# Attention in blocks of 32 queries by 64 keys ahead of an MLP: both heads of a pair in one pass, weights converted two blocks at a time, first stage in a written order

## The chip, the core and the metric

The kernel runs on one core of a Trainium2 chip. Times are device microseconds of that core, from launch to end, as the median of several executions. The core has a matrix engine (TensorE, PE in the profile, with its weight loads counted apart as PEld), three engines for everything else (VectorE or DVE, ScalarE or ACT, GpSimd or POOL), and an engine that issues the transfers (SyncE or SP). Each works through its own list of instructions in order; they wait for each other by semaphores.

## The reference: what is computed

Eight batches of eight heads, 576 tokens, 64 channels a head. Heads 0 to 3 see the last 32 tokens, heads 4 to 7 every fourth of the last 128. The heads' outputs side by side are a matrix of 4608 tokens by 512, and go through an MLP of 512 to 2048 to 512.

```python
rel = pos[:, None] - pos[None, :]
mask_plain = (rel >= 0) & (rel < window)                                    # window 32
mask_dil = (rel >= 0) & (rel < window * dilation) & (rel % dilation == 0)   # dilation 4
scores = scores - np.max(scores, axis=-1, keepdims=True)
attn = np.exp(scores)
attn = attn / (np.sum(attn, axis=-1, keepdims=True) + 1e-09)
...
h = x @ w_in
g = np.where(pos, h, np.where(neg, 0.0, (h + beta) ** 2 / (4.0 * beta)))   # pos: h >= 1, neg: h <= -1
return (g @ w_out).astype(np.float32)
```

The MLP's weights come as 64-bit floats.

## The kernel before

**MLP.** The 4608 tokens are nine tiles of 512, the 2048 hidden channels 16 blocks of 128. Activations and weights are held as two fp32r parts (high and rest), and each product of 128x128 by 512 columns is three matmuls: high by high, rest by high, high by rest. Layer 1 (line 396) takes 12 matmuls for a tile and a block, layer 2 (line 433) 12 as well: 3456 in all. A step s is one tile and one block: `layer1(s)`, then `layer2(s - 2)`. Between the two and behind the second, `run(2s)` and `run(2s + 1)` put in the pieces of attention that `place` has assigned to these slots. Between the layers the activation of a block is three passes on DVE (lines 410, 415, 419) and two on ACT (413, 416).

**Attention.** Heads 4 to 7 are re-arranged on the host so that a window is 32 neighbours there too. Queries go in tiles of 96, and each tile is scored against 128 keys, of which 32 to a query are in its window. The first 16 heads (two batches) are scored as plain fp32 matmuls (line 204), two heads in two row halves of the array. For the 48 later heads `split` cuts q and k into high and rest (lines 138 to 143), and line 227 scores a tile by one fp32r matmul of 96x256. DVE adds the mask (line 246), and a custom instruction for each tile (line 175) scales and takes the extreme at once; ACT makes the exp of each tile, with its sum (line 252); POOL multiplies by the inverse sums (line 285). DVE transposes the result in blocks of 32 (line 300, six for each head); for the first 16 heads PE does it (line 324). Line 358 multiplies by the values, 12 fp32 matmuls for a pair of heads, in two column halves. `store_x` then writes the high part (line 342, ACT) and the rest (line 343, DVE) into the tiles xh and xl, three of each, which layer 1 reads. A tile of 512 tokens is complete when the pair of heads 6 and 7 of its last batch is stored.

**Weights.** `fetch` brings a block (512 KB), and `weights` makes its two parts: ACT (line 115), ACT or DVE (121 or 123), a join of the two on DVE (126), the high part on ACT (131), the rest on POOL (132). 32 blocks are converted, in the steps of the first tile for the most part.

**What sets the order.** PE and SP run in program order all through. DVE, ACT and POOL are ordered by a scheduler, by priorities. `issue_after` holds the conversion of a block behind marks in ACT's and DVE's work. Eight heads are scored and transposed, and most of their values made, before layer 1 begins.

Of the kernel before, what the change touches and what calls it, by code (L numbers as in the profile page):

```python
# [6 lines left out]
F32 = mybir.dt.float32  # L23
# [4 lines left out]
ALU = mybir.AluOpType  # L28

# [3 lines left out]
QT, NQ = 96, 6  # L33
# [4 lines left out]
NF = DF // 128  # L38
NC = DM // 128
EPS = 1e-09  # L40
# [4 lines left out]
def body(ctx, tc, q, k, q2, k2, v, mask, eye, w_in, w_out, out):  # L45
# [7 lines left out]
    msk = const.tile([QT, 3, 128], F32, name="msk")  # L53
    ident = const.tile([QT, QT], F32, name="ident")
    consts = const.tile([128, 16], F32, name="consts")
    half_t = consts[:, 0:1]
    pts = [const.tile([128, NQ, QT], F32, name=f"pt{i}") for i in range(2)]
# [3 lines left out]
    nhead = B * H  # L61
    native = 2 * H

    spare = [f"{w}{f}" for f in range(NF // 2, NF) for w in ("wi", "wo")]

    def borrow(name):
        return pool.tile([128, 2 * DM], F32, tag=spare.pop(0), name=name)

    def load_pair(n):

        if 0 < n < H:
            qr, kr = borrow(f"qr{n}")[:, :S], borrow(f"kr{n}")[:, :KPAD]
        else:
            tags = ("qs", "kk") if n % 4 else ("qr", "kr")
            qr = pool.tile([128, S], F32, tag=tags[0], name=f"qr{n}")
            kr = pool.tile([128, KPAD], F32, tag=tags[1], name=f"kr{n}")
        nc.sync.dma_start(out=qr, in_=q[n // 2])
        nc.sync.dma_start(out=kr, in_=k[n // 2])
        for j in range(2):
            r = slice(64 * j, 64 * j + 64)  # L80
            heads[n + j] = dict(qs=qr[r], ks=kr[r])

    def load(n):
        qr = pool.tile([128, S], F32, tag="qr", name=f"qr{n}")
        kr = pool.tile([128, KPAD], F32, tag="kr", name=f"kr{n}")
        nc.sync.dma_start(out=qr, in_=q2[n - native])
        nc.sync.dma_start(out=kr, in_=k2[n - native])
        heads[n] = dict(qr=qr, kr=kr)

    def load_values(n):  # L90
        if 0 < n < H:
            vt = borrow(f"vt{n}")[:, : 2 * NQ * D]
        else:
            vt = pool.tile([128, 2 * NQ * D], F32, tag="vt", name=f"vt{n}", bufs=2)
        nc.sync.dma_start(out=vt, in_=v[n // 2])
        vt = vt.rearrange("p (j t d) -> p j t d", j=2, t=NQ)
        for j in range(2):
            heads[n + j]["vt"] = vt[:, j]

    wi, wo, raws = {}, {}, {}  # L100

    def fetch(f, src, name):

        raw = pool.tile([128, 2 * DM], U32, tag=f"{name}{f}", name=f"{name}_raw{f}")
        nc.sync.dma_start(out=raw, in_=src[:, f].bitcast(U32))
        raws[name, f] = raw

    def weights(f, w, name):

        raw = raws.pop((name, f))  # L110
        words = raw.rearrange("p (n x) -> p n x", x=2)
        low, high = words[:, :, 0], words[:, :, 1]
        m = pool.tile([128, DM], U32, tag="m", name=f"{name}_m{f}", bufs=3)

        nc.scalar.activation(
            out=m.bitcast(F32), in_=high.bitcast(F32), func=AF.Prelu, scale=2.0**-112, alpha=2.0**32
        )
        if name == "wi":

            top = raw.bitcast(U8).rearrange("p (n x) -> p n x", x=8)[:, :, 3]  # L120
            nc.scalar.activation(out=low, in_=top, func=AF.Copy, scale=1.0 / 32, bias=-31.0 / 64)
        else:
            nc.vector.tensor_scalar(
# [27 lines left out]
    def bank(n):  # L151

        if n > H:
            return "att", 2
# [527 lines left out]
```

## Time and profile before

| | |
|---|---|
| time, median of 3 executions | 948.66 us (948.19 to 948.94) |
| the profiled execution: span from the first to the last instruction | 945.8 us |
| granted TensorE clock over the span | 0.986 |
| layer 2 on PE, high part of the activations (line 433) | 385.8 us in 1152 |
| layer 1 on PE, high part (line 396) | 362.2 us in 1152 |
| exps on ACT (line 252) | 140.6 us in 360 |
| transposes on DVE (line 300) | 106.0 us in 288 |

For the profiled execution the profile has a span and no time of its own; the median of the other executions lies 2.9 us above that span. A row of the groups reads: line, engine, operation, what is written from what, shapes, count | busy us, mean ns of one | idle time before and what ended it. A matmul in fp32 leaves two records, each with a weight load; one in fp32r leaves one. Matmuls overlap in the array, so a record's length is more than the distance to the next start.

### The profile page before, as it was taken

The page shows a single profiled execution, that of the slowest core. Times are in us where ns is not written, and L with a number is a line of the kernel's source. Part 1 is how long each engine was busy: PE and PEld are TensorE (multiplying, and loading weights), DVE is VectorE, ACT ScalarE, POOL GpSimd, SP SyncE. Part 2 cuts the span into 40 slices and gives each one's busy share as a digit, 9 for nine tenths or more (in the row PEclk, how much of TensorE's full clock was granted, in tenths as well). Part 3 has the DMA queues.
Part 4 walks back from the last instruction along what each step waited for, and adds up shares of the span by engine and source line. Part 5 has one row for each costly group of instructions (what it writes and reads, how often), then busy time and mean ns, then how long its engine had stood idle before and what let it go on. Part 6 is the DMA issues. An engine that isn't in the chain of part 4 may idle for free.

```text
span 945.8 us, 14337 instructions
## 1 busy us (share of the span) xinstructions
PE 920.9 (97%) x4822; PEld 748.4 (79%) x4822; DVE 681.1 (72%) x1979; ACT 493.8 (52%) x1392; POOL 230.9 (24%) x148
## 2 busy tenths in 40 slices
PE   6679999999999999999999999999999999999998
PEld 5557788888888888888888888888888888888886
DVE  6788887888887788788887888888877643334333
ACT  6777876555565555555555555555655332222222
POOL 3454552222222222222222222222222000000000
PEclk8879999999999999999999999999999999999999
DMA  9961101322232113222322123222321010001001
GB/s 347 407 239 51 44 27 43 113 69 69 69 113 62 49 57 110 69 69 69 97 86 58 57 66 113 69 69 69 113 62 50 1 45 1 0 1 45 1 1 44
DMA packets 31017, 73.85 MB, mean 78 GB/s; under 512 B 3520, under 2 KB 3808, under 8 KB 30944
## 3 DMA queue, kind: packets, MB, share of 16 engines
q1 hardware_dynamic: 30944, 72.94, 23.7%
q8 instruction: 38, 0.62, 0.3%
q14 instruction: 35, 0.29, 0.1%
HBM read 63.49 MB, written 9.44 MB: 77 GB/s over the span
## 4 chain that ended last, share of the span: by engine, by line
PE 91%; ACT 4%; DVE 4%; DMA 1%; issue 1%; DVEq 0%; ACTq 0%
PE acc L433 41%; PE h L396 40%; PE o L358 4%; PE s L227 4%; ACT c L252 2%; DVE wi_m L126 1%; DMA wi_raw<-w_in 1%; DVE wo_m L126 1%; PE s L201 1%; DVE c L175 0%; ACT wi L131 0%; PE s L204 0%; PE t L324 0%; ACT xh L342 0%; DVE h L415 0%
## 5 line engine op out<-in xcount | busy, mean ns | idle before, releaser
L433 PE MATMUL acc<-wo,gh 128*128 128x512 f32 x1152 | 385.8, 396 | 4.1 <-ACT pt L326 4.1
L396 PE MATMUL h<-xh,wi 128*128 128x512 f32 x1152 | 362.2, 395 | 5.0 <-ACT xh L342 4.9
L433 PEld LDWEIGHTS acc<-wo,gh 128*128 128x128 f32 x1152 | 217.3, 189 | 52.8 <-ACT pt L326 4.3
L396 PEld LDWEIGHTS h<-xh,wi 128*128 128x128 f32 x1152 | 210.1, 189 | 47.4 <-ACT xh L342 5.3
L396 PE MATMUL h<-xl,wi 128*128 128x512 f32 x576 | 227.6, 395 | 0.0
L433 PE MATMUL acc<-wo,gl 128*128 128x512 f32 x576 | 226.0, 392 | 0.0
L252 ACT ACTIVATE c<-c 96x128 f32<-96x128 f32 x360 | 140.6, 393 | 117.9 <-DVE c L175 117.9
L143 POOL TENSOR_TENSOR kk<-kr,kk 128x608 fp32r<-128x608 f32 x48 | 95.3, 1985 | 422.8 <-ACT kk L139 422.8
L413 ACT ACTIVATE y<-y,consts 128x512 f32<-128x512 f32 x144 | 104.2, 724 | 123.6 <-DVE y L410 123.6
L416 ACT CAST gh<-h 128x512 fp32r<-128x512 f32 x144 | 84.6, 587 | 126.8 <-PE acc L433 122.1
L410 DVE TENSOR_SCALAR y<-h 128x512 f32<-128x512 f32 x144 | 99.3, 690 | 61.1 <-PE h L396 59.9
L415 DVE TENSOR_TENSOR h<-h,y 128x512 f32<-128x512 f32 x144 | 100.6, 699 | 52.8 <-ACT y L413 51.5
L396 PEld LDWEIGHTS h<-xl,wi 128*128 128x128 f32 x576 | 108.5, 188 | 25.5 <-DVE xl L343 0.2
L419 DVE TENSOR_TENSOR gl<-h,gh 128x512 fp32r<-128x512 f32 x144 | 98.8, 686 | 39.7 <-ACT gh L416 39.4
L433 PEld LDWEIGHTS acc<-wo,gl 128*128 128x128 f32 x576 | 108.8, 189 | 21.3
L300 DVE STREAM_TRANSPOSE pt<-c 32x192 f32<-32x192 f32 x288 | 106.0, 368 | 5.8
L246 DVE TENSOR_TENSOR c<-s,msk 96x256 f32<-96x256 f32 (+1 forms) x168 | 61.5, 377 | 39.6 <-PE s L227 38.6
L285 POOL TENSOR_TENSOR c<-c 96x768 f32<-96x768 f32 x56 | 82.6, 1477 | 21.0 <-DVE c L284 20.7
L175 DVE CUSTOM_DVE_ANT_0 c<-s,c 96x128 f32<-96x128 f32 x288 | 70.6, 281 | 1.0
L252 ACT ACTIVATION_READ_ACCUMULATOR c<-c 96x1 f32 x360 | 68.0, 189 | 0.0
L342 ACT CAST xh<-o 128x288 fp32r<-128x288 f32 (+8 forms) x112 | 38.4, 380 | 47.2 <-PE o L358 28.7
L227 PEld LDWEIGHTS s<-kk,qs 128*96 128x96 f32 x288 | 46.4, 161 | 15.7
(57 smaller groups left out, 632.8 us busy)
## 6 DMA issues: line engine op xcount, KB each, us to landing
kr<-k_in SPq DMA_DIRECT2D x56, 304.0 KB, 3.3
qr<-q_in SPq DMA_DIRECT2D x56, 288.0 KB, 2.8
vt<-v_in SPq DMA_DIRECT2D x32, 384.0 KB, 4.0
wi_raw<-w_in SPq DMA_DIRECT2D x16, 512.0 KB, 9.4
wo_raw<-w_in SPq DMA_DIRECT2D x16, 512.0 KB, 9.8
out<-out SPq DMA_DIRECT2D x32, 256.0 KB, 3.7
out<-outs SPq DMA_DIRECT2D x4, 256.0 KB, 2.0
msk<-mask_in SPq DMA_DIRECT2D x1, 144.0 KB, 3.6
```

The source lines that it names most:

```text
L143: nc.gpsimd.tensor_tensor(out=kk[:, 1], in0=hd["kr"], in1=kk[:, 0].bitcast(F32), op=ALU.subtract)
L227: PE.matmul(out=sv[:, t - t0], lhsT=hd["qs"][:, t * QT : (t + 1) * QT], rhs=hd["ks"][:, :, t * QT : t * QT + 128], start=True, stop=True,)
L252: last["act"] = nc.scalar.activation(out=c[:, t], in_=c[:, t], func=AF.Exp, bias=st[:, 0, t : t + 1], scale=-1.0, accum_out=st[:, 1, t : t ...
L285: nc.gpsimd.tensor_tensor(out=c, in0=c, in1=spread(st[:, 2]), op=ALU.mult)
L300: nc.vector.transpose(out=pt[r : r + 32, :, 32 * g : 32 * g + 32], in_=c[32 * g : 32 * g + 32, :, r : r + 32],)
L396: PE.matmul(out=hp, lhsT=wi[f][:, w, 128 * c : 128 * c + 128], rhs=x[:, c], start=c == 0 and i == 0, stop=c == NC - 1 and i == len(terms) - 1,
L410: nc.vector.tensor_scalar(out=y, in0=hp, scalar1=-1.0, scalar2=1.0, op0=ALU.max, op1=ALU.min)
L413: nc.scalar.activation(out=y, in_=y, func=AF.Square, bias=half_t, scale=0.5)
L415: activated = nc.vector.tensor_tensor(out=hp, in0=hp, in1=y, op=ALU.max)
L416: copied = nc.scalar.copy(out=gh, in_=hp)
L419: nc.vector.tensor_tensor(out=gl, in0=hp, in1=gh.bitcast(F32), op=ALU.subtract)
L433: PE.matmul(out=acc[m], lhsT=g[:, r], rhs=wo[f][:, w], start=f == 0 and i == 0, stop=f == NF - 1 and i == len(terms) - 1,)
```

## The change

- Queries go in blocks of 32, and each is scored against its 64 keys. The 18 blocks of a head are 18 fp32 matmuls of 64 rows by 32 columns with 64 moving columns; three blocks lie side by side in three column places, the two heads of a pair in the two row halves (line 126 of the new kernel). No head is split into high and rest any more.
- The softmax runs over both heads at once, 96 x 768: mask added (DVE, line 152 or 159), maximum (DVE, 170), subtraction (POOL, 174), one exp (ACT, 178), sums (DVE, 182), inverse, product (POOL, 188).
- The first eight pairs are transposed on PE as matmuls with an identity and multiplied by their values in 36 matmuls of 64x32; the 24 others are transposed on DVE, six instructions of 32x384 for a pair (line 211), and keep their 12 matmuls, now in turns between the heads.
- q and k of a pair come in one transfer, once, not doubled.
- Weights are fetched and converted two blocks at a time, 1024 columns a pass; all get the second ACT pass.
- Up to the first layer's start the order is written out for PE, SP, DVE, ACT and POOL. From there on, PE and SP are in program order as before, the others scheduled.

```diff
-QT, NQ = 96, 6
+QB, NB = 32, S // 32
+KW = 64
+EARLY = 8
...
+        for b in range(NB):
+            t, g = divmod(b, 3)
+            for j in range(2):
+                r = slice(64 * j, 64 * j + 64)
                 PE.matmul(
-                    out=sv[:, t - t0],
-                    lhsT=heads[m]["qs"][:, t * QT : (t + 1) * QT],
-                    rhs=heads[m]["ks"][:, t * QT : t * QT + 128],
+                    out=sps[j][QB * g : QB * g + QB, KW * t : KW * t + KW],
+                    lhsT=hd["q"][r, QB * b : QB * b + QB],
+                    rhs=hd["k"][r, QB * b : QB * b + KW],
...
+    def largest(n):
+        nc.vector.tensor_reduce(out=heads[n]["st"][:, 0], in_=heads[n]["c"], op=ALU.max, axis=AX.X)
+    def minus_largest(n, engine=nc.gpsimd):
+        c = heads[n]["c"]
+        engine.tensor_tensor(out=c, in0=c, in1=spread(n, 0), op=ALU.subtract)
+    def exp(n):
+        c = heads[n]["c"]
+        last["act"] = nc.scalar.activation(out=c, in_=c, func=AF.Exp, scale=1.0 / 8.0)
+    def sums(n):
+        c, st = heads[n]["c"], heads[n]["st"]
+        nc.vector.tensor_reduce(out=st[:, 1], in_=c, op=ALU.add, axis=AX.X)
+        nc.scalar.activation(out=st[:, 1], in_=st[:, 1], func=AF.Copy, bias=EPS)
+    def inverses(n, engine=nc.gpsimd):
+        c, st = heads[n]["c"], heads[n]["st"]
+        nc.vector.reciprocal(out=st[:, 2], in_=st[:, 1])
+        engine.tensor_tensor(out=c, in0=c, in1=spread(n, 2), op=ALU.mult)
...
+    def transpose(n):
+        c = heads[n]["c"].rearrange("p j t x -> p (j t) x")
+        pt = pts.rearrange("p j t i -> p (j t) i")
+        for g in range(3):
+            for h in range(2):
+                r = 32 * (g + h)
+                nc.vector.transpose(
+                    out=pt[r : r + 32, :, 32 * g : 32 * g + 32],
+                    in_=c[32 * g : 32 * g + 32, :, 32 * h : 32 * h + 32],
+                )
...
+        if n < EARLY:
+            for turn in range(2):
+                for i in range(half):
+                    for j in range(2):
+                        part = turn ^ j
+                        r = slice(64 * j, 64 * j + 64)
+                        at = half * part + i
+                        PE.matmul(
+                            out=ops[part][r, QB * i : QB * i + QB],
+                            lhsT=hd["v"][r, at],
+                            rhs=hd["pt"][r, QB * at : QB * at + QB],
...
+    def scaled(name, u):
+        ms[name, u] = pool.tile([128, 2, DM], F32, tag="m", name=f"m_{name}{u}", bufs=2)
+        nc.scalar.activation(
+            out=flat(ms[name, u]), in_=words_of(name, u)[1].bitcast(F32),
+            func=AF.Prelu, scale=2.0**-112, alpha=2.0**32,
+        )
...
+    for n in range(4, NP):
+        u = 8 * (n - 4) - 4
+        if n > 4:
+            place(u, lambda n=n: scores_step(n))
+            place(u + 1, lambda n=n: masks(n), lambda n=n: largest(n), lambda n=n: minus_largest(n))
+            place(u + 2, lambda n=n: exp(n))
+            place(u + 3, lambda n=n: sums(n))
+            place(u + 4, lambda n=n: inverses(n))
+        if n < EARLY:
+            place(u + 7, lambda n=n: transpose_pe(n))
         else:
+            place(u + 5, lambda n=n: transpose(n))
+        place(u + 10, lambda n=n: values_step(n))
+        place(u + 11, lambda n=n: stores(n))
...
+    with tc.manual_schedule(engines={eng.PE, eng.SP, eng.DVE, eng.Activation, eng.Pool}):
+        scores(0)
+        load_qk(4)
+        largest(0)
+        minus_largest(0, nc.vector)
+        exp(0)
...
+        layer1(0, 0, range(2))
+        layer1(0, 1, range(2))
+        values(2, (0, 1), store=False)
+        parts("wi", 1)
+        exp(4)
+        stores(2)
+        sums(4)
+        values(3, (2, 3), store=False)
+        fetch(("wi", 7), ("wo", 7))
+        scaled("wo", 0)
+        inverses(4)
+        stores(3)
+        top_bytes("wo", 0)
+        joined("wo", 0)
+        parts("wo", 0)
```

Three places of the order that follows. First PE in the long run, where a pair's scores come: before, two score matmuls (s from kk and qs) stand between the layers, here at the end of layer 1's block 4 (h from xh, xl and wi) and ahead of layer 2 (acc from wo, gh and gl).

```order
L396 MATMUL h_4_2959<-xh_853,wi_668 128x512 x2
L396 MATMUL h_4_2959<-xl_854,wi_668 128x512
L227 MATMUL s_2_2980<-kk_2871,qs_2870 96x256 x2
L433 MATMUL acc_0_2848<-wo_721,gh_2_2835 128x512
L433 MATMUL acc_0_2848<-wo_721,gl_2_2836 128x512
```

After, PE at the like place, at the end of layer 1's block 10:

```order
L377 MATMUL h_10_2176<-xh_381,wi_1048 128x512 x2
L377 MATMUL h_10_2176<-xl_382,wi_1048 128x512
L126 MATMUL s_2198<-qk_2027 32x64 x36
L412 MATMUL acc_0_1818<-wo_1131,gh_8_2116 128x512
L412 MATMUL acc_0_1818<-wo_1131,gl_8_2117 128x512
```

All 36 score matmuls of a pair stand in one place; before, they were six twos in six places.

Second, DVE in the first stage. Before, among the tiles' reduces (line 175, two instructions for each of the first heads' tiles, c from s and msk) the first sums and inverses stand where the scheduler put them:

```order
L175 ISA c_174<-s_4_194,msk 96x128
L175 ISA c_174 96x1
L271 TENSOR_SCALAR sums<-c_115 96x6
L175 ISA c_176<-s_4_195,msk 96x128
L175 ISA c_176 96x1
L175 ISA c_176<-s_4_195,msk 96x128
L175 ISA c_176 96x1
L276 RECIPROCAL c_115<-sums 96x6
```

After, DVE's first rows behind the memset are those of the written order (c_100 is pair 0, c_155 pair 1, qkc_74 pair 2):

```order
L152 TENSOR_TENSOR c_100<-s_101,msk 96x768
L170 TENSOR_REDUCE c_100<-c_100 96x12
L174 TENSOR_TENSOR c_100<-c_100 96x768
L150 TENSOR_TENSOR c_155<-s_0_156,msk 96x384
L150 TENSOR_TENSOR c_155<-s_1_157,msk 96x384
L170 TENSOR_REDUCE c_155<-c_155 96x12
L182 TENSOR_REDUCE c_100<-c_100 96x12
L150 TENSOR_TENSOR qkc_74<-s_2_200,msk 96x384
L150 TENSOR_TENSOR qkc_74<-s_3_201,msk 96x384
L187 RECIPROCAL c_100<-c_100 96x12
L170 TENSOR_REDUCE qkc_74<-qkc_74 96x12
L182 TENSOR_REDUCE c_155<-c_155 96x12
```

A pair's mask, maximum and sum are now single passes over both heads, and pair 1's mask and maximum stand between pair 0's subtraction and its sum.

Third, DVE where the last pair of a token tile is stored. Before (y, h and gl are the activation of block 15; xl_1935 is the tile that layer 1 takes up next, xl_2929 the one behind it; pt from c are the next head's transposes):

```order
L284 RECIPROCAL c_3552<-c_3552 96x6
L410 TENSOR_SCALAR y_15_3636<-h_15_3623 128x512
L343 TENSOR_TENSOR xl_1935<-o_0_3644,xh_1934 128x2x80
L415 TENSOR_TENSOR h_15_3623<-h_15_3623,y_15_3636 128x512
L343 TENSOR_TENSOR xl_1935<-o_1_3655,xh_1934 128x2x80
L343 TENSOR_TENSOR xl_2929<-o_0_3644,xh_2928 128x2x64
L300 STREAM_TRANSPOSE pt_67<-c_3552 32x6x32 x6
L343 TENSOR_TENSOR xl_2929<-o_1_3655,xh_2928 128x2x64
```

After, at the same boundary (xl_1889 is the tile that is taken up next, xl_2735 the one behind it; pts from c are the next pair's transposes):

```order
L394 TENSOR_SCALAR y_15_3318<-h_15_3305 128x512
L187 RECIPROCAL c_3250<-c_3250 96x12
L398 TENSOR_TENSOR h_15_3305<-h_15_3305,y_15_3318 128x512
L252 TENSOR_TENSOR xl_1889<-o_3326,xh_1888 128x2x80
L211 STREAM_TRANSPOSE pts<-c_3250 32x12x32 x6
L252 TENSOR_TENSOR xl_2735<-o_3326,xh_2734 128x2x64
L402 TENSOR_TENSOR gl_15_3320<-h_15_3305,gh_15_3319 128x512
L252 TENSOR_TENSOR xl_1889<-o_3326,xh_1888 128x2x80
L252 TENSOR_TENSOR xl_2735<-o_3326,xh_2734 128x2x64
```

The second store into the next tile stands behind the transposes, a store into the tile after it, and gl; before, both stood ahead of the transposes.

More of the change, by code (lines that the diff above doesn't have):

```diff
@@ L69, in load_pair @@
[L69 to L98, printed above, removed]
@@ L173, in reduce @@
[L173 to L203 removed]
+    small = const.tile([128, 96 + 64], F32, name="small")
@@ new lines, in body, with scores @@
+    last = {}
+    def scores(n, banks=None, add=True):
+        hd = heads[n]
+        if "c" not in hd:
+            hd["c"] = pool.tile([96, 832], F32, tag="c", name=f"c{n}", bufs=2)
+        cc = hd["c"]
+        c = hd["c"] = cc[:, :768].rearrange("p (j t x) -> p j t x", j=2, t=6)
+        hd["st"] = cc[:, 768:804].rearrange("p (s j t) -> p s j t", s=3, j=2)
+        both, sps = banks_of(banks, f"s{n}")
+        if n == 0:
+            ones = half_t.broadcast_to([128, 128])
+            for _ in range(11):
+                PE.matmul(out=sps[0][:, :128], lhsT=ones, rhs=ones, start=True, stop=True)
+        for b in range(NB):
+            t, g = divmod(b, 3)
+            for j in range(2):
+                r = slice(64 * j, 64 * j + 64)
@@ L328, in body, with transpose_pe @@
-    last = {}
+    def transpose_pe(n, banks=None, copy=True):
+        c = heads[n]["c"]
+        both, tps = heads[n]["t"] = banks_of(banks, f"t{n}")
+        for t in range(6):
+            for j in range(2):
+                PE.matmul(
+                    out=tps[t // 3][64 * j : 64 * j + 64, 96 * (t % 3) : 96 * (t % 3) + 96],
+                    lhsT=c[:, j, t],
+                    rhs=ident,
+                    start=True,
+                    stop=True,
+                )
+        if copy:
+            copies(n)
@@ L547, in behind @@
+    def behind(marks, *steps):
         with tc.issue_after(marks[0].ins), tc.issue_after(marks[1].ins):
-            for name, f in blocks:
-                weights(f, {"wi": wi, "wo": wo}[name], name)
-    def marks():
-        return last["act"], last["dve"]
+            for fn, name, u in steps:
+                fn(name, u)
     def run(u):
@@ new lines, in body @@
+        parts("wi", 1)
[10 more added lines that the diff above has]
+        parts("wo", 0)
+        ready = last["act"], last["dve"]
+    with tc.manual_schedule(engines={eng.PE, eng.SP}):
+        steps = [(t, f) for t in range(NT) for f in range(NF)]
+        for s in range(len(steps) + 2):
+            if s < len(steps):
+                layer1(*steps[s], range(2, NC) if s < 2 else range(NC))
+                activation(*steps[s])
@@ L613, in body @@
             run(2 * s)
-            while l2 <= s - lag and l2 < len(steps):
-                layer2(*steps[l2])
-                l2 += 1
+            if s < len(todo):
+                behind(last["g", s - 1] if s else ready, (weights, *todo[s]), (parts, *todo[s]))
+            if s >= 2:
+                layer2(*steps[s - 2])
             run(2 * s + 1)
-        assert not slots
+        assert not slots, slots.keys()
 def kernel(q, k, v, moe_w_in, moe_w_out):
```

661 lines of the change are left out of this document (281 added, 380 removed).

## The prediction

> **What bounds the kernel now.** I read the page from the top (share of each engine, the 40 slices, the chain that ended last), then the table of stretches, then the chain and the timeline at the places that the change touches.
>
> ```profile
> span 945.8 us, 14337 instructions
> PE 920.9 (97%) x4822; PEld 748.4 (79%) x4822; DVE 681.1 (72%) x1979; ACT 493.8 (52%) x1392; POOL 230.9 (24%) x148
> PE   6679999999999999999999999999999999999998
> PE 91%; ACT 4%; DVE 4%; DMA 1%; issue 1%; DVEq 0%; ACTq 0%
> ```
>
> TensorE is the bound: it is 91% of the chain, and of its 40 slices only the first three are not full. So time can be saved in two ways only: TensorE starts its long run earlier, or it has less to do in it.
>
> ```profile
> 0.00:25.00 25.00, 17.29 (x146) 14.59 (x148) 17.19 (x115) 16.52 (x59) 8.86 (x10) 0.88 0.94 350
> 25.00:50.00 25.00, 17.71 (x171) 14.38 (x171) 17.45 (x62) 17.98 (x58) 12.14 (x9) 0.84 1.03 408
> 50.00:75.00 25.00, 19.36 (x102) 14.84 (x99) 21.96 (x51) 20.32 (x56) 11.41 (x8) 0.80 0.62 215
> 75.00:100.00 25.00, 25.00 (x150) 19.87 (x149) 18.69 (x53) 20.06 (x56) 10.92 (x9) 1.00 0.17 54
> 300.00:325.00 25.00, 25.00 (x133) 20.35 (x133) 19.96 (x63) 13.44 (x41) 6.92 (x4) 1.00 0.23 66
> ```
>
> The columns are the stretch, its length, the busy time of PE, its weight loads, DVE, ACT and POOL, the granted clock, the DMA share and GB/s. From 75 us on PE is full at the full clock. Before that it is busy 54.4 of 75 us, at 0.80 to 0.88 of the clock. How little of the MLP is done there shows when the stretches are asked for line 396 (first layer) and then for line 433 (second layer) alone:
>
> ```profile
> 0.00:75.00 75.00, 14.36 (x48) 0.84 0.86 324
> 800.00:925.00 125.00, 65.85 (x268) 1.00 0.03 9
> 0.00:75.00 75.00, 6.56 (x18) 0.84 0.86 324
> 800.00:925.00 125.00, 66.47 (x276) 1.00 0.03 9
> ```
>
> Late in the run, without attention, 268+276 matmuls take 125 us: 0.230 us each. By 75 us only 48+18 = 66 have started, 15.2 us of work. All 3456 matmuls of the MLP stay as they are, 795 us at that pitch.
>
> **The start.** What holds it back is in the chain of waits of the first 75 us (start, length, what; my choice of its pieces):
>
> ```profile
> 7.07 8.97 ACT c L252 x46
> ...
> 41.46 4.63 ACT c L252 x24
> ...
> 47.34 1.66 PE h L396 x3
> ...
> 56.02 8.05 DMA wi_raw<-w_in
> ...
> 65.29 3.21 DVE wo_m L126
> 68.50 2.96 DVE wi_m L126
> ```
>
> The exps of single tiles on ACT take 9.0 us, later ones (for heads 8 and 9) 4.6 us more just before the last stores of the first token tile, so layer 1 goes on only at 47.34. Then the weights are late, by a transfer and two slow joins. The change takes up each of these: one exp per pair, all engines in a written order, weights two blocks at a time and fetched earlier. Prices for its wide passes exist in the trace, from the few heads which were done so already, and for the conversion in its old width:
>
> ```profile
> L274 DVE TENSOR_TENSOR c<-c,sums 96x768 f32<-96x768 f32 x4 | 3.8, 948 | 0.1
> L292 DVE TENSOR_REDUCE c<-c 96x6 f32<-96x768 f32 x4 | 3.7, 934 | 0.0
> L291 ACT ACTIVATE c<-c 96x768 f32<-96x768 f32 x4 | 3.3, 840 | 1.0 <-POOL c L290 1.0
> L285 POOL TENSOR_TENSOR c<-c 96x768 f32<-96x768 f32 x56 | 82.6, 1477 | 21.0 <-DVE c L284 20.7
> L126 DVE SCALAR_TENSOR_TENSOR wi_m<-wi_m,wi_raw 128x512 uint32<-128x512 uint32 x16 | 16.5, 1035 | 2.1 <-ACT wi_raw L121 0.9 <-issue 0.8 <-ACT wi_m L115 0.4
> L343 DVE TENSOR_TENSOR xl<-o,xh 128x288 fp32r<-128x288 f32 (+8 forms) x112 | 41.4, 384 | 18.7 <-ACT xh L342 18.0
> ```
>
> In the written order DVE does, up to the last store of tile 0: five mask adds and one subtraction at 0.95 us (5.7), five maxima and five sums at 0.93 (9.3), five reciprocals (about 1), two joins over 1024 columns at 1.3 to 2.1 (3.4) and 14 stores at 0.25 to 0.45 (about 5). That is 24 us, from about 6.7 us on, when the first scores are there: 31 us if it never waits, which is the lower end. It waits: pair 3's sum stands behind POOL (subtractions and products of pairs 0 to 3, seven passes at 1.48 us, in order) and behind ACT, whose conversions stand between the exps. Following the three orders row by row, with these durations, I find pair 3's sum at about 25 us, pair 1's stores at 29, pair 4's maximum at 32, then the twelve or so matmuls of layer 1 that are ready, the values of pairs 2 and 3, and the last store at about 42, where the old kernel got on at 47.34 and only after that had the rest of its tile. The first block of the second layer's weights is converted at 49, so little is lost there; in the old kernel the waits went on to 72. The DMA engines were nearly full in the first 50 us, but the change needs about 8 MB up to that block, at 350 GB/s some 24 us, so they don't set it.
>
> From 42 to 75 us there are 33 us. Two bursts of scores, two of transposes and one of values of the later pairs (7.4 by the prices below) and about a microsecond of waiting for the second layer's weights go off; 24.6 us are 107 matmuls, with the twelve 119, call it 120 by 75 us in place of 66: 54 x 0.230 = **-12.4 us**. The ends: 0 if the weights take the wait over, -20 if DVE hardly waits.
>
> **Scores and values in the long run.** PE's timeline for one pair before (start, length, what):
>
> ```profile
> 300.06 0.39 PE L433 MATMUL acc<-wo,gh 128*128 128x512 f32 x1
> 300.29 0.40 PE L227 MATMUL s<-kk,qs 128*96 128x256 f32 x2
> 300.53 0.62 PE L396 MATMUL h<-xh,wi 128*128 128x512 f32 x2
> ...
> 303.08 0.40 PE L396 MATMUL h<-xl,wi 128*128 128x512 f32 x1
> 303.40 1.43 PE L358 MATMUL o<-pt,vt 128*64 128x96 f32 x24
> 304.76 0.50 PE L433 MATMUL acc<-wo,gh 128*128 128x512 f32 x1
> 305.10 0.39 PE L433 MATMUL acc<-wo,gl 128*128 128x512 f32 x1
> ```
>
> Two score matmuls add 300.53 - 300.06 - 0.23 = 0.24 us; a pair has six such twos, 1.45 us. The values add 305.10 - 303.08 - 2 x 0.23 = 1.56 us. A pair costs 3.0 us, 24 late pairs 72 us.
>
> After, a pair's scores are 36 fp32 matmuls of 64 rows by 32 columns, in six places of the array. An fp32 matmul leaves two records (12 matmuls of line 204 are 24 records), so the burst has 72. The nearest row is that of line 204, fp32 in two row groups:
>
> ```profile
> 35.70 1.55 PE L204 MATMUL s<-kr,qr 64*96 64x128 f32 x24
> 37.18 0.73 PE L396 MATMUL h<-xh,wi 128*128 128x512 f32 x2
> ...
> 66.91 0.66 PE L324 MATMUL t<-ident,c 96*128 96x96 f32 x6
> 67.35 0.71 PE L396 MATMUL h<-xh,wi 128*128 128x512 f32 x2
> ```
>
> 24 records of 128 moving columns take 1.48 us to the next start, 0.062 each with two places at work, so half of that for 64 columns: 72 x 0.031 = 2.2 us if only two places ever work together, and 0.74 if all six do. Line 324 (one place, 96 columns) takes 0.44/6 = 0.073 per record, while line 358's 24 records of 96 columns in two column groups take 1.36 us, 0.057 each: column groups overlap as row groups do. No row shows both at once. I take 1.4 us: 24 x (1.4 - 1.45) = **-1.2 us**; ends -17 and +18.
>
> The values of late pairs are the same 12 matmuls, but now change column group after every one instead of after three. I take 1.35 for 1.56, as two groups then start side by side: 24 x -0.21 = **-5 us**; ends -12 (each group wholly beside the other) and 0.
>
> The first eight pairs' remains after 75 us: before, 48 records of line 204 (3.0 us), 36 of line 324 (2.6) and three bursts of values (4.7), 10.3 in all, by the counts that these lines have in the stretches after 75 us. After, one burst of scores (1.4), two of 24 transposing records (2.7) and three values of 72 records of half a column block's length at about 1.9 (between the 24 records' 1.36 and twice that): 9.8. **-0.5 us**; ends -4 and +4.
>
> DVE's load falls (a wide mask add, maximum and sum, 2.8 us a pair, for 12 custom reduces, six adds and two subtractions), and ACT's too, so neither comes near the bound; the conversions hide behind the MLP as before.
>
> **A new wait.** In the change's order on DVE the six transposes of the next pair, now over both heads, stand between the stores of the pair that completes a token tile, and two other passes stand ahead of the last store that layer 1 needs. Before, all that was needed stood ahead of the transposes. The trace at such a boundary:
>
> ```profile
> 354.56 1.47 POOL L285 TENSOR_TENSOR c<-c 96x768 f32<-96x768 f32 x1
> 356.84 2.28 DVE L300 STREAM_TRANSPOSE pt<-c 32x192 f32<-32x192 f32 x6
> 359.77 0.68 DVE L419 TENSOR_TENSOR gl<-h,gh 128x512 fp32r<-128x512 f32 x1
> 360.66 0.40 PE L396 MATMUL h<-xl,wi 128*128 128x512 f32 x1
> ```
>
> After, the transposes start when POOL's product is done, about 356.2. Six at twice the width take 2.28 to 4.56 us; at 3.8 they end at 360.0, and a store (0.4), gl (0.68) and the store that is needed (0.4) end at 361.5. PE wants it at 360.66 less the 0.24 of scores that no longer stand there: 1.1 us late. Six boundaries (tiles 1 to 6; behind the last there is no pair to transpose): **+6.5 us**, ends 0 and +11.
>
> **Sum**: -12.4 - 1.2 - 5 - 0.5 + 6.5 = -12.6 on the span of 945.8, so 933.2. The median of the runs shown, 948.66, is 2.9 above that span, as the start and end of the launch lie around it. Forecast **936.1 us**.
>
> **Rivals.** *PE keeps the order of small matmuls.* Then a block's second record waits for its first, and only then does the next place start: 36 x 0.062 = 2.2, with 0.4 for entering and leaving (the values' 1.56 above their own 1.18 or so): 2.6 us a burst. 27 bursts (24 and three early) at 1.2 more: +32, **968 us**, slower. It decides once a burst is above 1.85 us. Against it speaks line 358: its groups stand six records by six, and strictly in order they would take about 24 x 0.073 = 1.75, not 1.36. For it: nothing here has changed place at every matmul in six places. The Trainium skill, "TensorE: Matmul & The Clock Gate", section "Part 3: Packing small matmuls — row/col tiling", says that matmuls start and end strictly in program order; by that rule the sum is this rival's, and line 358's row speaks against it in that form.
>
> *PE can't be fed.* A burst has 72 weight loads and 72 matmuls; the densest rows here are one record per 0.057 us. At that pace it takes 4.1 us: 27 x 2.7 = +73, **1009 us**. Against it: both dense rows are explained by the array's own time. The same page, section "Wait — 56ns, not 53.3ns?", gives a floor of about 25 ns between starts, and about 62 ns where the sequencer decodes in software; an estimate from these is 1.8 or 4.5 us a burst, and no row here shows which holds.
>
> *The start doesn't gain.* ACT has three passes for a conversion where it had two or three, in an order that lets none step ahead; if the first blocks come as late as before, the wait only changes its name: 0 to 2 of the 12.4 us, **948 us**.
>
> *All places overlap and no boundary waits*: 1.1 us a burst, 27 x -0.3 and -6.5: **922 us**.
>
> **How the numbers follow.** Chances: forecast 0.48 (its own range 920 to 947), order kept 0.17, not fed 0.07, no gain at the start 0.14, better case 0.14. About 0.2% (1.9 us) is what a measurement can tell from no change. Faster by more: 0.43 + 0.14 + some of the start rival (0.05) = 0.62; within: 0.08; slower: both PE rivals, the rest of the start's and the forecast's edge, 0.30. The range leaves out 1009 and most below 917: 917 to 970.
>
> **What would show it.** About 120 MLP matmuls by 75 us, the first of the second layer before 52; a score burst of 72 records between 1.1 and 1.75 us from neighbour to neighbour; values at 1.35; waits of layer 1 for xl of about a microsecond at six tile boundaries and nowhere else. Wrong would be: a burst over 1.85, PE waiting for wi or wo after 55 us, or DVE or ACT between PE's matmuls all through the run.

## The result, and the profile after

The changed kernel takes **933.38 us** (median of 4 executions, 932.57 to 933.93), the kernel before 948.42 beside it on the same chip: ratio 0.9842, 95% interval 0.9828 to 0.9855. The forecast was 936.1. So the sum came out right, but the table at the end of this section shows that it was right because large errors of both signs cancelled.

The page after: span, engines, PE's 40 slices and the chain that ended last.

```profile
span 931.5 us, 16485 instructions
PE 902.9 (97%) x7126; PEld 734.3 (79%) x7126; DVE 534.6 (57%) x854; ACT 323.2 (35%) x544; POOL 131.9 (14%) x84
PE   6979999999999999999999999999999999999998
PE 85%; DVE 7%; ACT 3%; DMA 3%; POOL 1%; issue 1%; SPq 0%; ACTq 0%; POOLq 0%
```

The span is 14.3 us shorter. DVE, ACT and POOL lost 147, 171 and 99 us of work, nearly thirty times as much together, and almost all of it lay beside PE. PE is still the bound. The table of stretches, with the columns of before:

```profile
0.00:25.00 25.00, 16.45 (x430) 15.07 (x430) 13.79 (x20) 8.52 (x14) 8.89 (x10) 0.79 0.94 363
25.00:50.00 25.00, 19.82 (x354) 17.23 (x353) 9.79 (x20) 11.96 (x25) 9.10 (x5) 0.70 1.01 424
50.00:75.00 25.00, 22.99 (x230) 17.97 (x230) 17.63 (x25) 21.30 (x30) 14.23 (x7) 0.82 0.55 212
```

PE is busier than before in the second and third stretch, but between 25 and 50 us its clock is granted at 0.70, where it was 0.84. What it got done of the MLP is shown by the stretches asked for line 377 (layer 1, two rows) and then for line 412 (layer 2):

```profile
0.00:75.00 75.00, 18.05 (x53) 0.77 0.83 333
800.00:925.00 125.00, 63.42 (x264) 1.00 0.02 9
0.00:75.00 75.00, 6.05 (x24) 0.77 0.83 333
800.00:925.00 125.00, 68.74 (x289) 1.00 0.02 9
```

By 75 us 53 + 24 = 77 matmuls have started, against 66 before and the 120 of the prediction. And from 800 to 925 us there are 264 + 289 = 553 where before there were 544: a matmul of the MLP now takes 0.226 us and not 0.230. The same operation got faster, which no step of the prediction had foreseen.

PE's timeline in the long run, at one pair's values and, 18 us on, at another's scores:

```profile
323.56 0.39 PE L377 MATMUL h<-xl,wi 128*128 128x512 f32 x1
323.88 1.21 PE L277 MATMUL o<-pts,v 128*64 128x96 f32 x24
325.02 0.50 PE L412 MATMUL acc<-wo,gh 128*128 128x512 f32 x1
325.36 0.40 PE L412 MATMUL acc<-wo,gl 128*128 128x512 f32 x1
...
341.29 0.39 PE L377 MATMUL h<-xl,wi 128*128 128x512 f32 x1
341.60 0.97 PE L126 MATMUL s<-qk 64*32 64x64 f32 x72
342.50 0.50 PE L412 MATMUL acc<-wo,gh 128*128 128x512 f32 x1
342.85 0.40 PE L412 MATMUL acc<-wo,gl 128*128 128x512 f32 x1
```

The values add 325.36 - 323.56 - 2 x 0.23 = 1.34 us, where they added 1.56. The scores add 342.85 - 341.29 - 0.46 = 1.10, where six twos added 1.45. The 72 records themselves run from 341.60 to 342.50: 12.5 ns each.

A tile boundary, the one that the prediction looked at. In the timeline the number in brackets is the idle time ahead of a row, and what ended it:

```profile
351.67 3.47 DVE L211 STREAM_TRANSPOSE pts<-c 32x384 f32<-32x384 f32 x6
...
355.17 0.38 DVE L252 TENSOR_TENSOR xl<-o,xh 128x128 fp32r<-128x128 f32 x1
...
355.59 0.45 ACT L251 CAST xh<-o 128x160 fp32r<-128x160 f32 x1 [2.56 <-DVE xl L252]
...
356.09 0.74 PE L377 MATMUL h<-xh,wi 128*128 128x512 f32 x2 [1.64 <-ACT xh L251]
```

PE waits for ACT's xh. ACT waits for DVE's subtraction of the piece before it, and that stands behind the six transposes. The list of PE's waits over the whole run shows how often (total us, times, longest):

```profile
PE h L377 <- ACT xh L251: 12.0, 6, 4.0
...
PE h L377 <- DVE gl L402: 2.0, 1, 2.0
PE h L377 <- DVE xl L252: 1.0, 1, 1.0
```

The second of these lines belongs to the start, and so does one of the six waits of the first, 4.0 us. The other five, with the one for xl, are the six boundaries: 9.0 us idle, 10.0 if one measures from a matmul's start to the next one's start and takes off the usual 0.23, since a record's length covers a part of each gap.

Where the 14.3 us of the span went, each term measured from the starts of neighbouring matmuls of the MLP, as a mean over all its places (the start is what is left over):

| term | predicted | measured |
|---|---|---|
| start, first eight pairs, tail | -12.9 | -1.8 |
| scores of 24 late pairs | -1.2 | 24 x (1.10 - 1.46) = -8.6 |
| values of 24 late pairs | -5.0 | -5.4 |
| six tile boundaries | +6.5 | +10.0 |
| pitch of layer 1 | 0 | 1728 x (226.7 - 231.6 ns) = -8.5 |
| sum | -12.6 | -14.3 |

The first row holds 11 more matmuls by 75 us, which are 2.5 us, and whatever the other rows don't name; layer 2's pitch is in it too, which fell by up to 0.9 ns (1.6 us).

### The profile page after: what moved, and what is told of

It is laid out like the page before. It is cut to its first block, busy times and chain, and to the rows that moved or that the text cites. A ratio compares the mean times of both kernels' runs of the same rounds, so it can differ in the third digit from the quotient of the medians.

```text
span 931.5 us, 16485 instructions
## 1 busy us (share of the span) xinstructions
PE 902.9 (97%) x7126; PEld 734.3 (79%) x7126; DVE 534.6 (57%) x854; ACT 323.2 (35%) x544; POOL 131.9 (14%) x84
## 4 chain that ended last, share of the span: by engine, by line
PE 85%; DVE 7%; ACT 3%; DMA 3%; POOL 1%; issue 1%; SPq 0%; ACTq 0%; POOLq 0%
PE acc L412 40%; PE h L377 39%; PE s L126 2%; PE o L277 2%; DVE pts L211 2%; DMA qk<-qk_in 2%; PE o L267 1%; POOL c L174 1%; ACT y L397 1%; DVE y L394 1%; DVE h L398 1%; DMA qkc<-qk_in 1%; DVE xl L252 1%; DVE c L182 1%; DVE c L170 1%
## 5 line engine op out<-in xcount | busy, mean ns | idle before, releaser
L377 PEld LDWEIGHTS h<-xh,wi 128*128 128x128 f32 x1152 | 217.2, 189 | 62.3 <-ACT xh L251 14.4
L397 ACT ACTIVATE y<-y,small 128x512 f32<-128x512 f32 x144 | 104.3, 724 | 238.9 <-DVE y L394 238.6
L174 POOL TENSOR_TENSOR c<-c 96x768 f32<-96x768 f32 x29 | 42.6, 1470 | 471.6 <-DVE c L170 463.7
L211 DVE STREAM_TRANSPOSE pts<-c 32x384 f32<-32x384 f32 x144 | 81.8, 568 | 2.5 <-POOL pts L455 0.7
L252 DVE TENSOR_TENSOR xl<-o,xh 128x288 fp32r<-128x288 f32 (+8 forms) x112 | 42.9, 384 | 21.2 <-ACT xh L251 20.3
L188 POOL TENSOR_TENSOR c<-c 96x768 f32<-96x768 f32 x30 | 44.2, 1473 | 70.5 <-DVE c L187 70.5
L182 DVE TENSOR_REDUCE c<-c 96x12 f32<-96x768 f32 x30 | 28.4, 947 | 33.7 <-ACT c L178 33.7
L178 ACT ACTIVATE c<-c 96x768 f32<-96x768 f32 x30 | 25.3, 844 | 42.9 <-POOL c L174 35.2
L126 PEld LDWEIGHTS s<-qk 64*32 64x32 f32 x2160 | 24.8, 107 | 13.7 <-issue 9.9
L126 PE MATMUL s<-qk 64*32 64x64 f32 x2160 | 29.7, 223 | 3.3 <-DMA qk<-qk_in 3.3
## 6 DMA issues: line engine op xcount, KB each, us to landing
vp<-v_in SPq DMA_DIRECT2D x3, 576.0 KB, 12.5
```

The source lines that it names most:

```text
L126: PE.matmul(out=sps[j][QB * g : QB * g + QB, KW * t : KW * t + KW], lhsT=hd["q"][r, QB * b : QB * b + QB], rhs=hd["k"][r, QB * b : QB * b ...
L174: engine.tensor_tensor(out=c, in0=c, in1=spread(n, 0), op=ALU.subtract)
L188: engine.tensor_tensor(out=c, in0=c, in1=spread(n, 2), op=ALU.mult)
L211: nc.vector.transpose(out=pt[r : r + 32, :, 32 * g : 32 * g + 32], in_=c[32 * g : 32 * g + 32, :, 32 * h : 32 * h + 32],)
L252: last["dve"] = nc.vector.tensor_tensor(out=dst(xl[:, c]), in0=src, in1=dst(xh[:, c]).bitcast(F32), op=ALU.subtract)
L377: PE.matmul(out=hp, lhsT=weight("wi", f, w, slice(128 * c, 128 * c + 128)), rhs=x[:, c], start=c == 0 and i == 0, stop=c == NC - 1 and i = ...
```

## The start, as the trace after shows it

PE in the first 50 us:

```profile
16.05 2.19 PE L221 MATMUL t<-small,c 96*64 96x96 f32 x24 [2.03 <-POOL c L188]
18.91 2.19 PE L221 MATMUL t<-small,c 96*64 96x96 f32 x24 [0.67 <-POOL c L188]
21.03 4.05 PE L267 MATMUL o<-pts,v 64*64 64x32 f32 x72
...
31.12 2.19 PE L221 MATMUL t<-small,qkc 96*64 96x96 f32 x24
34.50 1.52 PE L126 MATMUL s<-qk 64*32 64x64 f32 x72 [1.20 <-DMA qk<-qk_in]
35.95 1.22 PE L377 MATMUL h<-xh,wi 128*128 128x512 f32 x2
...
40.02 4.39 PE L267 MATMUL o<-vp 64*64 64x32 f32 x144
...
49.55 1.22 PE L377 MATMUL h<-xh,wi 128*128 128x512 f32 x2 [3.97 <-ACT xh L251]
```

Three things stand in it. From 16 to 33.3 us PE has little but small matmuls, and they run at half the clock, as stretches of 2.5 us show (the last three columns are the granted clock, the DMA share and GB/s):

```profile
20.00:22.50 2.50, 2.50 (x42) 2.28 (x42) 1.17 (x2) 1.48 (x3) 0.76 (x2) 0.50 1.02 430
...
27.50:30.00 2.50, 2.50 (x52) 2.50 (x52) 0.00 (x0) 2.50 (x5) 1.98 (x1) 0.50 1.01 425
...
37.50:40.00 2.50, 2.50 (x10) 1.75 (x8) 0.61 (x1) 0.22 (x1) 1.72 (x2) 0.83 1.02 423
```

PE is busy all through these stretches and yet gets 0.50. The clock goes up only in the stretch that begins 1.6 us after layer 1's matmuls of 128x512 have begun. Second, the scores of pair 4 wait for their queries and keys. Third, layer 1 does twelve matmuls, then the values of pairs 2 and 3 and three more of layer 1 follow, and it goes on at 49.55, after a wait of 3.97 us for the stores of pair 3; the prediction had put that at 42. What these stores wait for stands in the timeline of DVE and ACT:

```profile
37.16 0.95 DVE L170 TENSOR_REDUCE c<-c 96x12 f32<-96x768 f32 x1
...
45.43 0.94 DVE L182 TENSOR_REDUCE c<-c 96x12 f32<-96x768 f32 x1
...
46.52 1.10 ACT L334 ACTIVATE m_wo<-raw_wo 128x1024 f32<-128x1024 f32 x1
...
47.53 0.60 ACT L251 CAST xh<-o 128x256 fp32r<-128x256 f32 x1
...
49.52 0.61 DVE L252 TENSOR_TENSOR xl<-o,xh 128x256 fp32r<-128x256 f32 x1 [0.26 <-ACT xh L251]
```

Pair 4's maximum (line 170) only begins at 37.2, because its scores were late; its sum (182) and a conversion of weights (334) stand ahead of pair 3's stores (251, 252), and the last of these begins at 49.52.

After that wait nine matmuls of 128x128 by 512 run at half the clock too. Behind the transposes that follow, PE waits once more, for the first activation of the MLP:

```profile
50.00:52.50 2.50, 2.50 (x7) 1.88 (x7) 1.62 (x4) 2.33 (x4) 0.00 (x0) 0.50 1.02 430
...
55.00:57.50 2.50, 0.72 (x12) 0.53 (x8) 1.58 (x3) 2.50 (x4) 2.43 (x2) 0.91 1.04 437
...
57.74 0.73 PE L377 MATMUL h<-xh,wi 128*128 128x512 f32 x2 [2.01 <-DVE gl L402]
```

The clock is back at 0.91 in a stretch in which PE is busy for only 0.72 of 2.5 us, which reads as if the grant came late, for work done before; no run tests that. Layer 2 begins at 63.14, where the prediction had it before 52.

## The experiments

**Why layer 1 got faster.** First idea: x's and the weights' operands became aligned to 128 bytes in SBUF. One kernel takes that away in the new kernel, one gives it to the old one. A second idea: the banks of PSUM into which layer 1 writes.

```diff
 new kernel (e1)
-const.tile([128, 96 + 64], F32, name="small")
+const.tile([128, 96 + 80], F32, name="small")
 old kernel (e2)
-const.tile([128, 16], F32, name="consts")
+const.tile([128, 32], F32, name="consts")
 new kernel (e3), behind the definition of bank()
+    for i in (4, 5):
+        bank(i, f"first{i}")
```

> The changed kernel with 64 bytes more in its first constant tile, so that every tile behind it in SBUF starts at 64 modulo 128 bytes, as all of them did in the old kernel, and not at 0. In the old kernel the matmuls of layer 1 start 231.6 ns apart on average, in the new one 226.7, with the same operands. Theory 'alignment' (a matmul is slowed by its operands' place in SBUF): layer 1's distance goes up to about 231.6 ns, and the time by 1728 x 5 ns, some 8 us, to about 941 to 942. Theory 'bank' (the old kernel's h lay in PSUM banks 0 and 1, the new one's in 6 and 7): nothing changes, 933.4 within 1 us. Theory 'load' (less other work on the engines): nothing changes either.

> The old kernel with 64 bytes more in its small constant tile, so that the tiles behind it start at 0 modulo 128 bytes. Theory 'alignment': layer 1's matmuls come 226.7 ns apart in place of 231.6, and the time falls by about 8 us to 940. Theories 'bank' and 'load': 948.4 within 1 us, layer 1 at 231.6.

> The changed kernel with h in PSUM banks 0 and 1, as in the old kernel, the attention's pair of banks moved to 2 and 3. Theory 'bank': layer 1 goes from 226.7 to about 231.6 ns a matmul, the time to about 941. Theories 'alignment' and 'load': 933.4 within 1 us, layer 1 stays at 226.7.

Measured: e1 934.03 us (ratio 0.9852, 0.9837 to 0.9867) with layer 1 still at 226.7 ns; e2 948.25 (0.9999, 0.9990 to 1.0008) with 231.6; e3 933.71 (0.9846, 0.9831 to 0.9861) with 226.7. Neither the alignment nor the bank matters: both ideas fall.

What does differ is the distance between the two operands that PE reads at once, the moving one and the weights that are loaded for the next matmul. From the places of the operands in a partition of SBUF and the starts of the matmuls of the last tiles, mean ns to the next start by that distance modulo 256 bytes (count in brackets where both occur). e5 and e6 are the two experiments that follow:

```
          layer 1                        layer 2
before    128: 232.0                     0: 228.7
after       0: 226.7                     0: 227.8
e5          0: 227.0                     0: 227.1
e6          0: 227.1 (409)               0: 227.9 (635)
          128: 232.2 (288)             128: 232.6 (80)
```

The rows of e5 and e6 are the test: e5 puts 384 unused bytes between x and all that lies behind it in the old kernel, the weights among it, so that the distance becomes a multiple of 256; e6 spreads the buffers of x in the new one, so that some of them lie at 128.

```diff
 old kernel (e5), behind the tiles of x
+    pad = pool.tile([128, 96], F32, tag="pad", name="pad")
 new kernel (e6), where there are three buffers
-return pool.tile([128, 4, TOK], dt, tag=tag, name=name, bufs=bufs)
+both = pool.tile([128, 4 * TOK + 32], dt, tag=tag, name=name, bufs=bufs)
+return both[:, : 4 * TOK].rearrange("p (a x) -> p a x", a=4)
```

> The old kernel with an unused tile of 384 bytes between the x tiles and everything behind them, so that the weights lie at another distance from x: 1024 modulo 2048 bytes in place of 640 (in the changed kernel it is 0). Theory 'relative place' (a matmul is slowed when the address of its moving operand and that of the weights loaded beside it stand in some bad relation): layer 1's matmuls go from 231.6 towards 226.7 ns, the time to about 940. Rival, 'not the place in SBUF': 231.6 ns and 948.2 within 1 us.

> The changed kernel with 128 bytes more for each of the six x buffers, so that the distance between x and the weights takes other values, differing from buffer to buffer (0 modulo 2048 in the changed kernel; here multiples of 128 bytes). Theory 'relative place': layer 1's mean distance differs from one token tile to the next, in steps up to about 5 ns, as the tiles use the buffers in turn. Rival: 226.7 ns in every tile, and a time like the changed kernel's, 933 to 934.

Measured: e5 939.2 us (938.33 to 939.46; ratio 0.9902, 0.9887 to 0.9917), e6 one run at 937.91 with a span of 935.8. In e5 the stretch from 800 to 925 us, line 396 and then line 433, has 276 + 278 = 554 matmuls, as many as the new kernel:

```profile
800.00:925.00 125.00, 66.29 (x276) 1.00 0.02 9
800.00:925.00 125.00, 66.17 (x278) 1.00 0.02 9
```

The old kernel becomes 9.4 us faster by an unused buffer alone. In e6 both pitches appear in one run, sorted by the distance. The pitch of layer 1 came with the change as an accident of allocation, and the distance of the operands is its cause. Why the hardware prefers one distance, these runs don't show. Nor do they explain the smaller differences at the same distance: layer 2 lies between 227.1 and 228.7 at 0.

**The boundary.** The transposes are put behind the last store in DVE's order.

```diff
-            place(u + 5, lambda n=n: transpose(n))
+            place(u + 5, lambda n=n: transpose_behind(n))
...
+    def transpose_behind(n):
+        with tc.issue_after(last["dve"].ins):
+            transpose(n)
```

> The changed kernel with the six transposes of a late pair held behind the last store of the pair before it. Theory 'the transposes stand in the way of the stores': the six waits of layer 1 at tile boundaries (1.1 to 1.9 us each, 10 us in all in the trace of the changed kernel) go away but for what the cut-up stores need by themselves, and the time falls by 8 to 10 us, to 923.5 to 925.5. Theory 'the chain of stores is itself too long' (ACT's cast, DVE's subtraction, four times in turn): the waits stay at a microsecond or more each, and the time at 930 or above.

Measured: 923.55 us (ratio 0.9739, 0.9723 to 0.9755), 9.8 less than the changed kernel, against 10.0 counted at the boundaries. So the waits are real time on the path, and the transposes' place is their cause. e12 below has the same edit, and of its waits of layer 1 for xh and xl only one is left, at 47.2 us in the start:

```profile
PE h L377 <- ACT xh L251: 0.3, 1, 0.3
```

**What makes the score burst short.** The same 36 matmuls, written place by place instead of changing place at each.

```diff
-        for b in range(NB):
-            t, g = divmod(b, 3)
-            for j in range(2):
-                r = slice(64 * j, 64 * j + 64)
+        for g, j in [(g, j) for g in range(3) for j in range(2)]:
+            r = slice(64 * j, 64 * j + 64)
+            for t in range(6):
+                b = 3 * t + g
```

> The changed kernel with the same 36 score matmuls of a pair written place by place (six blocks of one place of the array, then six of the next) in place of changing place at every matmul. Theory 'places overlap, but PE looks only a few records ahead': one place works at a time for most of the burst, 72 records at 0.05 to 0.062 us less a little, so a burst takes 3 to 4 us in place of 0.90 (from its start to the next matmul's), and the time rises by 28 late bursts x 2.1 to 3.1, to 990 to 1020. Theory 'the burst is limited by how fast PE is fed, or PE looks far ahead': the order doesn't matter, 0.9 us and 933 to 934.

PE's timeline of one burst:

```profile
370.21 3.24 PE L126 MATMUL s<-qk 64*32 64x64 f32 x72
373.38 0.50 PE L412 MATMUL acc<-wo,gh 128*128 128x512 f32 x1
```

3.17 us from start to start in place of 0.90, and 995.04 us for the kernel (one run): 27 bursts at 2.27 us more are 61.3 of the 61.7 us. All six places do work side by side, but only if neighbouring matmuls in the program's order lie in different places. The starts of the single records in this trace show how much overlap is left: inside one place they lie 56 ns apart, so 72 one after another would take 4.03 us. The burst is 0.86 us shorter, 0.17 for each of its five changes of place, so a new place begins about three records before the old one is done. An estimate from the same 56 ns, with all six places at work all through, is 0.67 us; the changed kernel's 0.90 comes near it. How far PE looks ahead is read from these bursts alone and was not tried apart. The Trainium skill, "TensorE: Matmul & The Clock Gate", "Part 3: Packing small matmuls — row/col tiling", has matmuls start and end strictly in program order. Read as the prediction's first rival read it, so that a block's second record and every place behind it wait for the first, it gives 2.2 us and more; 0.90 speaks against that reading, while e9's 3.17 shows that the order of the places still counts.

**The start.** Three edits: e8 brings pair 4's queries and keys ahead of five fetches of weights; e7 does the same and lets PE multiply a constant tile where it would idle, ahead of scores 1 to 3 and transposes 0 and 1, to raise the clock early (this work has no part in the output); e10 leaves DVE, ACT and POOL to the scheduler in the first stage, as they were before the change.

```diff
 e8 (and e7)
         scores(0)
         load_qk(4)
+        fetch(("wi", 1), ("wo", 0), ("wi", 2), ("wo", 1), ("wi", 3))
 e7, and a like one ahead of the transposes
+        if n in BUSY_S:
+            keep_busy(sps[0], BUSY_S[n])
 e10
-with tc.manual_schedule(engines={eng.PE, eng.SP, eng.DVE, eng.Activation, eng.Pool}):
+with tc.manual_schedule(engines={eng.PE, eng.SP}):
```

(The same fetch stood ahead of this block and is taken from there.)

> The changed kernel with two edits of its first stage: idle stretches of PE between 6 and 16 us filled with matmuls of constants (7, 2 and 10 ahead of the scores of pairs 1 to 3, 9 and 3 ahead of the transposes of pairs 0 and 1), whose results the real ones overwrite, and pair 4's q and k fetched ahead of the five large weight transfers. Theory 'PE at half clock and the transfer of pair 4 set the start': the half-clock stretch from 13.7 to 38.4 us disappears for the most part, the first matmul of layer 1 comes at 26 to 31 us in place of 35.95, and the time falls by 4 to 8 us, to 925.5 to 929.5. Rival 'the softmax chain on DVE, ACT and POOL sets the start': the clock changes, layer 1 still begins after 34 us, and the time stays within 1.5 us of 933.4.

> The changed kernel with pair 4's q and k fetched ahead of the five large weight transfers, and nothing else. PE's own work at half clock ends at about 33.3 us there, 1.2 us before the scores of pair 4 start, so the theory of the run before (half clock and transfer together) says 0 to -1.5 us, 932 to 933.4. If the transfer alone set the start, layer 1 would begin several microseconds earlier and the time fall by 3 us or more.

> The changed kernel with DVE, ACT and POOL left to the scheduler in the first stage too (PE and SP in program order as before). If the written order earns its place, layer 1 goes on later than at 49.6 us and the time rises by 2 to 6 us, to 935 to 939. If PE at half clock and the transfers set the start, whatever the others do, it stays within 1.5 us of 933.4.

Measured: e8 931.95 us (ratio 0.9828, 0.9813 to 0.9842), e7 935.12 (0.9859, 0.9843 to 0.9876), e10 927.73 (0.9784, 0.9768 to 0.9801). In e8 PE's timeline has no wait for the transfer any more, and layer 1 begins at 34.81 in place of 35.95:

```profile
33.36 1.52 PE L126 MATMUL s<-qk 64*32 64x64 f32 x72 [0.23 <-PE t L221]
34.81 1.22 PE L377 MATMUL h<-xh,wi 128*128 128x512 f32 x2
```

So the transfer costs about 1.4 us (the intervals of the two ratios overlap, but in the traces layer 1 begins 1.1 and layer 2 1.5 us earlier, the latter at 61.68 in place of 63.14). What then stands just ahead of these scores are the small matmuls at half clock. e7 should have halved their time and missed. PE's timeline of e7 (its line 115 is the added work, 232 and 278 are lines 221 and 267 of the others):

```profile
13.29 4.09 PE L115 MATMUL s<-small 128*128 128x128 f32 x20
...
21.05 1.21 PE L232 MATMUL t<-small,c 96*64 96x96 f32 x24
...
24.20 2.29 PE L278 MATMUL o<-pts,v 64*64 64x32 f32 x72
27.56 2.19 PE L232 MATMUL t<-small,qkc 96*64 96x96 f32 x24 [1.07 <-POOL qkc L197]
29.68 4.05 PE L278 MATMUL o<-pts,vp 64*64 64x32 f32 x72
```

The clock came (transposes 1.21 us instead of 2.19, values 2.29 instead of 4.05), but the added work at 13.29 ran mostly at half clock itself, 0.20 us a record where the 14 at 7.26 took 0.13, and stood in front of real work, and at 27.56, after PE had idled for 1.07 us, the clock was down again and stayed down with small matmuls. Layer 1 began at 38.25. By its rows four transposes and two values at half clock cost 7.4 us of PE's time. That the start would gain as much at full clock is not shown: this way of filling idle time did not save it, and no other was tried.

e10 was expected to be slower or the same, and is 5.7 us faster. In its timeline layer 1 goes on at 46.22 where it went on at 49.55:

```profile
46.22 0.73 PE L377 MATMUL h<-xh,wi 128*128 128x512 f32 x2 [0.26 <-ACT xh L251]
```

Pair 4's sum is done there at 42.7, ahead of the stores, and the conversion of line 334 begins at 46.47, when layer 1 already goes on; so the stores follow their values at once. This is so although layer 1's first matmul comes 1.2 us later, at 37.14. PE idles less, and from 47.5 us its clock stays at 1.00 until it next waits; in the changed kernel it is 0.50 from 50.0 to 52.5. By 75 us 66 + 36 = 102 matmuls of the MLP have started, 25 more than the 77: 25 x 0.227 = 5.7, all of the gain.

**The edits together.** e11 has e4, e8 and an order written by hand with the stores of pair 3 ahead of pair 4's sum, and a conversion of weights held back a step; e12 has e4, e8 and e10.

```diff
 e11, beside the edits of e4 and e8
         stores(2)
-        sums(4)
         values(3, (2, 3), store=False)
+        stores(3)
+        sums(4)
...
-        stores(3)
...
-behind(last["g", s - 1] if s else ready, 
+behind(last["g", max(s - 1, 0)], 
```

> The changed kernel with four edits: a late pair's transposes behind the stores of the pair before it (923.6 alone), pair 4's q and k ahead of the large weight transfers (-1.4 alone), the stores of pair 3 written straight behind those of pair 2 in the first stage, ahead of pair 4's sum and a weight conversion, and the first conversion of the long run held behind the first activation of the MLP. If the waits of layer 1 at 45 to 50 us (4.0 us, for the stores of pair 3) and at 55.7 to 57.7 (2.0 us, for the first activation, which stands behind conversions on ACT) are set by that order, they shrink to about 2 and 0 us, and the time is 917 to 920. If they are set by something else (PE's values at half clock, the halved clock behind each wait), it is 921 to 923.

> The changed kernel with DVE, ACT and POOL left to the scheduler in the first stage (927.7 alone), the late pairs' transposes behind the stores of the pair before (923.6 alone, -9.8), and pair 4's q and k ahead of the large weight transfers (-1.4 alone). If the three gains lie in different places they add up: 927.7 - 9.8 - 0 to 1.4, that is 916.5 to 918. If the scheduler's gain and that of the earlier transfer overlap fully and the transposes meet a new wait, it is 919 or more.

Measured: e11 919.12 us (ratio 0.9693, 0.9679 to 0.9708), e12 917.61 (0.9673, 0.9656 to 0.9690). In e11 the wait for the stores of pair 3 shrinks from 4.0 to 1.6 us, so most of it came from the written order; the wait for the first activation grows from 2.0 to 2.9, so holding back that conversion did not help. The gains of the single edits, 9.8 + 1.4 + 5.7 = 16.9, would make 916.5 of 933.38; 917.61 is measured, so they nearly add. e12 has the lowest time, 3.3% below the kernel before and 1.7% below the changed one:

```profile
span 915.8 us, 16490 instructions
PE 899.1 (98%) x7126; PEld 734.9 (80%) x7126; DVE 535.8 (59%) x854; ACT 319.4 (35%) x544; POOL 132.7 (14%) x84
```

## Why the prediction was right in its sum and wrong in most of its terms

That the sum came within 3 us is luck. The start and the boundaries were too hopeful by 11.1 and 3.5 us; the scores, the values and the pitch came out 7.4, 0.4 and 8.5 us better than forecast.

- **The bound**: right. PE stays it, and of the work taken from DVE and ACT nothing appears in the time except at the start and the boundaries.
- **The start, -12.4**: wrong. The step that failed is "Following the three orders row by row, with these durations, I find [...] pair 4's maximum at 32, [...] and the last store at about 42". The maximum came at 37.2 and the last store at 49.5, and by 75 us 11 more matmuls had started, not 54. The runs show two causes and leave a third argued. The argued one: the prediction's prices for bursts of small matmuls, 1.35 us for transposes and 1.9 for values, lie near the full clock, while the trace gives 16.9 us for four and two of them where e7's rows would make 9.4. "So they don't set it" was wrong for pair 4's transfer, which waits its turn behind fetches of weights: the total of megabytes was counted, and not what stands ahead of the one transfer that matters (e8: 1.4 us). And the written order puts pair 3's stores behind pair 4's sum, a row that was read but timed 7.5 us too early (e10: 5.7 us). The rival "The start doesn't gain" is nearly what happened to this term, with 2.5 us by 75: its "order that lets none step ahead" is what e10 undoes, while its "three passes for a conversion" were not tried.
- **Scores, -1.2**: right mechanism, wrong size; 1.10 us a pair where 1.4 was taken. Between ends of 0.74 and 2.2 about the middle was taken, as no row had six places at work; the burst is 0.90 long, near the end where all six work, and entering and leaving adds 0.2. "Only two places ever work together" is refuted by the trace. "PE can't be fed" is refuted as well: 0.90 us a burst, 12.5 ns a record, is below its 4.1 and below both estimates that stand with it. "PE keeps the order" would have needed a burst above 1.85.
- **Values, -5**: right, 1.34 us measured for 1.35, -5.4.
- **The new wait, +6.5**: right in its place, too small. Priced was DVE's own chain to the rest (xl); the trace shows a longer one, in turns: subtraction of one piece, then ACT's cast of the next, then PE. The waits are 1.1 us at the first boundary and 1.7 to 1.85 at the others. e4 takes them away for 9.8.
- **The MLP's pitch**: "All 3456 matmuls of the MLP stay as they are, 795 us at that pitch." They stayed, and the pitch did not: -8.5 us by where the buffers happened to fall. Without that, the same change would have come out near 942 us; the prediction had no term for it.

Left open: what raises and lowers PE's clock while it is busy. The trace shows 0.50 with small matmuls and 1.00 a little after wide ones began at 35.95, but 0.50 again for the nine wide ones behind the wait at 49.55; e7 shows both with small ones. How much of the array has to be at work, and for how long, was not tried.

## What to carry to other kernels

When small matmuls go to several places of the array, write them so that neighbours change place, and price them from a burst of the same kind, not from a two-place one. At each point where the bound engine waits for a whole chain of other engines, walk that chain piece by piece, since two engines in turns cost the sum of both; long passes that nobody needs soon belong behind it. And before explaining a small gain by an edit, look whether an operation that was not edited has changed its own pitch.

## What the hardware showed that was not expected

- A matmul of 128x128 by 512 columns in fp32r takes about 227 ns from start to start if the moving operand and the weights lie a multiple of 256 bytes apart in SBUF, and 232 at 128 modulo 256 (e5, e6).
- PE was granted half its clock for 17 us of nearly unbroken small fp32 matmuls. It came up some 2.5 us after the first matmuls of 128x128 by 512; after a wait of 4.0 us nine more of these ran at half clock for 4 us.
- 72 records of 64x32 by 64 columns take 0.90 us in six places by turns and 3.17 place by place, where those of one place start 56 ns apart.
